# Filter and row loads moved to ScalarE's queue, and unread products cut into quarters of the array

## The chip, the cores and the metric

The kernel runs on one core of a Trainium2 chip. The time is that of the device, in microseconds (us), from the first to the last instruction of one execution. TensorE (PE) multiplies matrices, VectorE (DVE), ScalarE (ACT) and GpSimd (POOL) do element-wise work, and SyncE (SP) issues transfers. ScalarE and GpSimd issue transfers as well, each from its own instruction queue, in the order of its instructions.

## The reference

```python
def _attn_ref(x, filt_r, filt_i):            # x: (8, 3136, 256), filters: (1569, 256)
    X = np.fft.rfft(x, axis=1)
    F = (filt_r + 1j * filt_i)[None, :, :]
    return np.fft.irfft(X * F, n=x.shape[1], axis=1).astype(np.float32)

def _moe_ref(x, w_in, w_out, g_ln):          # x: (25088, 256), w_in: (256, 1024), w_out: (1024, 256)
    h = x @ w_in
    e = np.exp(h - np.max(h, axis=-1, keepdims=True))
    solu = h * (e / (np.sum(e, axis=-1, keepdims=True) + 1e-09))
    mu = np.mean(solu, axis=-1, keepdims=True)
    var = np.mean((solu - mu) ** 2, axis=-1, keepdims=True)
    ln = (solu - mu) / np.sqrt(var + 1e-06) * g_ln
    return (ln @ w_out).astype(np.float32)
```

The first function filters each of 8 entries along its 3136 positions; the second is applied to all 8 x 3136 = 25088 rows of the result.

## The kernel before

The Fourier transform of length 3136 is done in two stages, 49 x 64, as products with tables. `first` multiplies a piece of x (98 rows of 4 x 256 values, loaded by `fetch_x`) by the first table (PE `pa`), and `store_first` writes the result to d1 in device memory. `forward` multiplies a unit of d1 (read by `fetch` as t2) by the second table (PE `pb`), `turn` and `multiply` apply the filters (DVE `p`, `i`), `inverse` goes back (PE `pc`), and `store` writes to d2. `fetch_back` loads a piece of d2 and `back` multiplies it by the last table (PE `py`), which gives `y`, the input of the second function. The second function's products are PE `m` (with w_in) and PE `o` (with w_out).

The 8 entries are taken in five groups. Group 0 is done alone, ahead of everything else. It ends with ten products whose result nobody reads, and with the last table's products for entry 0:

```python
        start(0)
        for i in range(NS):
            sp.turn(i)
            sp.multiply(i, (0, 1))
            if i + 1 < NS:
                start(i + 1)
            last = sp.prods[i]
            sp.inverse(i, nc.scalar.copy)
            sp.store(i, nc.gpsimd.dma_start)

        for j in range(10):
            idle = ps_h.tile([P, 2, 512], FP32, name=f"idle_{j}", tag="h")
            nc.tensor.matmul(out=idle[:, 0, :], lhsT=tables[NS // NG - 1][:, 0, 0, :],
                             rhs=last.rearrange("p b c -> p (b c)"), start=True, stop=True)
        for j in (4, 5):
            begin(j)
        for ch in range(NH // NCH):
            fetch_back(0, ch, pools["r"])
            for cb in range(KD):
                back(0, ch, cb, nc.scalar.copy)
        # ... (the last weights are converted)
```

The loads of the row pieces, from SyncE, and of the filters for groups 1 to 4, from GpSimd:

```python
        def fetch_x(self, i, split=by_16):
            b, ch = divmod(i, NH // NCH)
            self.xs[i] = self.pools["r"].tile([P, NCH, C], FP32, name=f"x_{self.n}_{i}", tag="r")
            split((nc.sync.dma_start, nc.sync.dma_start), self.xs[i][0:NR],
                  x[self.entries[b]].rearrange("(r n) c -> r n c", n=NH)[
                      :, NCH * ch:NCH * ch + NCH, :])

    def fetch_back(e, ch, rows_pool, split=by_16):
        n, b = next((n, g[0].index(e)) for n, g in enumerate(GROUPS) if e in g[0])
        t4s[e, ch] = rows_pool.tile([P, NCH, C], FP32, name=f"t4_{e}_{ch}", tag="r")[0:NK]
        split(
            (nc.sync.dma_start, nc.sync.dma_start), t4s[e, ch],
            d2[n][b].rearrange("s (a n) c -> (s a) n c", a=4)[:, NCH * ch:NCH * ch + NCH, :])

    def load_filter(s, count):
        f = fpool.tile([P, 2, 2, C], FP32, name=f"f_{s}", tag="f")
        for p in range(2):
            nc.gpsimd.dma_start(out=f[NQ * p:NQ * p + NQ, 0:count],
                                in_=f_dram[s:s + count].rearrange("s q k c -> q s k c"))
        return f
```

After that come 196 steps (and a tail), one for each 128 rows of the second function. Two steps make a pair: 7 products with w_in and 28 with w_out. The work of groups 1 to 4 is spread over the steps. In a step `t` with a piece of x or of d2, its products run; in a step with a unit of a spectrum, `pb` runs, and `pc` one step later. All loads of pieces share three buffers (pool "r"), so a load is placed at the end of step `at`, which depends on when the piece three places back is used:

```python
        for i, t in enumerate(spread(pieces, *first_at)):
            row_loads.append((t, lambda sp=sp, i=i: sp.fetch_x(i, whole)))
            # ... first, store_first
        for i, t in enumerate(spread(len(sp.units), *spectrum_at)):
            ahead(t, 2).append(lambda sp=sp, i=i: sp.fetch(i, nc.scalar.dma_start))
            ahead(t, 1).append(lambda sp=sp, i=i: sp.fetch_filter(i))
            ahead(t, 2).append(lambda sp=sp, i=i: sp.fetch_de(i))
            # ... forward and turn in step t, multiply and inverse in t + 1, store in t + 2
    # ...
            row_loads.append((t, lambda e=e, ch=ch: fetch_back(e, ch, pools["r"], whole)))
    # ...
    row_loads.sort(key=lambda load: load[0])
    for n, (t, load) in enumerate(row_loads):
        at = max(t - 3, row_loads[n - 3][0] if n >= 3 else -1)
        assert at < t
        if at < 0:
            load()
        else:
            loads[at].append(load)
```

The order inside a step, cut to what matters here (`first_of` holds the products of pieces in the first nine steps, `early` and `late` hold them afterwards; `keep` and `keep_out` are ScalarE's copies of m and o):

```python
    def step(k):
        # ...
        for job in stores[k] + products[0][k] + first_of[k]:
            job()
        # product(j, 1), keep, project(p, 5), keep_out, product(j, 2)   (even k; odd: product(j, 5), keep)
        # turn(k - 3), regroup(j - 3, 0): SyncE's transfers solu_t<-turn
        # ... finish: VectorE's part of m and o
        exponential(k - 2)                       # ScalarE
        for job in early[k]:
            job()
        # ... the other products, regroup(j - 3, 1), project_sums: GpSimd's additions
        normalize(k - 2)                         # VectorE, then a square on ScalarE
        # ... finish, store_out: SyncE's transfers out_dram<-ot
        for job in mid[k] + late[k] + loads[k]:
            job()
```

Of the kernel before, what the change touches and what calls it, by code (L numbers as in the profile page):

```python
# [24 lines left out]
NS, NQ = (N1 + 1) // 2, 64  # L25
NR = 2 * N1
NK = 4 * NS
NG = 5
# [52 lines left out]
def kernel(  # L81
# [10 lines left out]
    nc = tc.nc  # L92
# [5 lines left out]
    def pool(name, bufs, space=None, stack=ctx):  # L98
        kw = {} if space is None else {"space": space}
        return stack.enter_context(tc.tile_pool(name=name, bufs=bufs, **kw))  # L100
# [51 lines left out]
    class Spectrum:  # L152
# [14 lines left out]
                return ap[:, s, :, :].rearrange("b p c -> p b c")  # L167
            return ap[0, s:s + count, :, :].rearrange("s p c -> p s c")

        def fetch_x(self, i, split=by_16):  # L170
            b, ch = divmod(i, NH // NCH)
            self.xs[i] = self.pools["r"].tile([P, NCH, C], FP32, name=f"x_{self.n}_{i}", tag="r")
            split((nc.sync.dma_start, nc.sync.dma_start), self.xs[i][0:NR],
                  x[self.entries[b]].rearrange("(r n) c -> r n c", n=NH)[
                      :, NCH * ch:NCH * ch + NCH, :])

# [84 lines left out]

    t4s = {}

    def fetch_back(e, ch, rows_pool, split=by_16):

        n, b = next((n, g[0].index(e)) for n, g in enumerate(GROUPS) if e in g[0])
        t4s[e, ch] = rows_pool.tile([P, NCH, C], FP32, name=f"t4_{e}_{ch}", tag="r")[0:NK]
        split(
            (nc.sync.dma_start, nc.sync.dma_start), t4s[e, ch],
            d2[n][b].rearrange("s (a n) c -> (s a) n c", a=4)[:, NCH * ch:NCH * ch + NCH, :])  # L270

    def back(e, ch, cb, evac):

        ps = ps_t.tile([P, 512], FP32, name=f"py_{e}_{ch}_{cb}", tag="t")
        psv = ps[:, 0:NCH * NR].rearrange("p (n r) -> p n r", r=NR)
        for i in range(NCH):
            nc.tensor.matmul(out=psv[:, i, :], lhsT=t4s[e, ch][:, i, cb * P:cb * P + P],  # L277
                             rhs=wi_t, start=True, stop=True)
        n0, t0 = NCH * ch, e % 2 * S
        evac(out=y[:, cb, t0:t0 + S].rearrange("p (r n) -> p n r", n=NH)[:, n0:n0 + NCH, :], in_=psv)  # L280


    with ExitStack() as st:
        pools = {name: pool(name + "0", bufs, stack=st)
                 for name, bufs in (("r", 6), ("t1", 4), ("t2", 5), ("p", 2), ("g", 3))}
# [34 lines left out]
        filters, tables = {}, {}  # L320
# [28 lines left out]
        sp = Spectrum(0, pools, resident, lambda s, count: tables[s // NG][:, s % NG:s % NG + count])  # L349
# [27 lines left out]
        for i in range(NS):  # L377
# [4 lines left out]
            last = sp.prods[i]  # L382
# [2 lines left out]

        for j in range(10):
            idle = ps_h.tile([P, 2, 512], FP32, name=f"idle_{j}", tag="h")
            nc.tensor.matmul(out=idle[:, 0, :], lhsT=tables[NS // NG - 1][:, 0, 0, :],
                             rhs=last.rearrange("p b c -> p (b c)"), start=True, stop=True)
        for j in (4, 5):  # L390
            begin(j)
        for ch in range(NH // NCH):
# [3 lines that stand above are left out]
# [10 lines left out]
    def psum(kind, name):  # L406
        return {"b": ps_b, "t": ps_t}[kind].tile([P, 2, C], FP32, name=name, tag=kind)
# [7 lines left out]
    pools = {name: pool(name + "1", bufs)  # L415
             for name, bufs in (("r", 3), ("t1", 3), ("t2", 2), ("p", 2), ("g", 2))}
# [3 lines left out]
    def load_filter(s, count):  # L420
        f = fpool.tile([P, 2, 2, C], FP32, name=f"f_{s}", tag="f")
        for p in range(2):
            nc.gpsimd.dma_start(out=f[NQ * p:NQ * p + NQ, 0:count],
                                in_=f_dram[s:s + count].rearrange("s q k c -> q s k c"))
        return f

# [223 lines left out]
    def spread(count, start, over):  # L650
        return [start + i * over // count for i in range(count)]

    def ahead(t, by):
        return loads[max(0, t - by)]
# [9 lines left out]
    row_loads = []  # L664

    for n in range(1, len(GROUPS)):
        entries, first_at, spectrum_at = GROUPS[n]
        sp = Spectrum(n, pools, load_filter, load_de)
        pieces = len(entries) * NH // NCH
        for i, t in enumerate(spread(pieces, *first_at)):  # L670
            row_loads.append((t, lambda sp=sp, i=i: sp.fetch_x(i, whole)))
            for u in range(2):
                (first_of if t < LAG else (early, late)[u])[t].append(lambda sp=sp, i=i, u=u: sp.first(
                    i, (u,), psum("t", f"pa_{sp.n}_{i}_{u}").rearrange("p a c -> p (a c)").rearrange(
                        "p (o n) -> p o n", o=1), nc.scalar.copy))
                (first_of[t] if t < LAG else mid[t] if u == 0 else stores[t + 1]).append(
                    lambda sp=sp, i=i, u=u: sp.store_first(i, 2 * u, nc.gpsimd.dma_start))
# [4 lines that stand above are left out]
            early[t].append(lambda sp=sp, i=i: sp.forward(i, psum("b", f"pb_{sp.n}_{i}")))  # L682
            early[t].append(lambda sp=sp, i=i: sp.turn(i, bufs=1))
            for part in range(2):
                products[part][t + 1].append(lambda sp=sp, i=i, part=part: sp.multiply(i, (part,)))
            late[t + 1].append(lambda sp=sp, i=i: sp.inverse(i, nc.scalar.copy))
            stores[t + 2].append(lambda sp=sp, i=i: sp.store(i, nc.gpsimd.dma_start))
    for e in range(1, B):


        start, end = (-(-S * (e - 1) // P) + 1) // 2 * 2 + (2 if e == 3 else 0), S * e // P // 2 * 2 - 2
        for ch, t in enumerate(spread(NH // NCH, start, end - start)):
            row_loads.append((t, lambda e=e, ch=ch: fetch_back(e, ch, pools["r"], whole)))
            for cb in range(KD):
                (first_of if t < LAG else (early, late)[cb])[t].append(
                    lambda e=e, ch=ch, cb=cb: back(e, ch, cb, nc.scalar.copy))
# [133 lines left out]
```

## Time and profile before

| | |
|---|---|
| time, median of 3 runs | 1791.7 us (1790.85 to 1792.85) |
| span of the profiled run | 1779.0 us |
| PE busy | 1671.6 us, 94% |
| DVE, ACT, POOL busy | 1244.1, 1068.4, 1093.9 us |
| mean DMA throughput | 177 GB/s, 314.57 MB |
| filter loads f<-f_dram, GpSimd | 152, 128 or 256 KB each |
| piece loads in the steps, SyncE | 48 of x (392 KB), 56 of d2 (400 KB) |
| unread products | 10, as 20 records, 8.7 us busy by the page's groups |

A profile's page gives busy times and their share of the span, then the span in 40 equal slices, each digit being tenths of a slice (9 is 90% or more). "PEclk" is the granted clock of TensorE in tenths of full speed. The chain follows the work that ended last backwards, at each step to what released it. A line of a group reads: source line, engine, operation, output<-inputs, shape, count, busy time, mean ns of one, idle time ahead of it and who ended that. A line of a timeline starts with start and length in us, and ends with the idle time before it and its releaser. Matmul records overlap, since a matmul's record includes its latency: the rate is read from start to start. An fp32 product of 512 columns is two records. Names like t, d, f and x are the tiles' names without numbers; t<-d is a piece or a unit that is read back, f<-f_dram a filter load.

### The profile page before, as it was taken

What the parts mean: (1) busy time and instruction counts of PE and PEld (TensorE: products, weight loads), DVE (VectorE), ACT (ScalarE), POOL (GpSimd) and SP (SyncE); (2) the same over time, 40 slices, a digit from 0 to 9 for tenths busy, and PEclk for the clock granted to TensorE, in tenths of its full rate; (3) what the DMA queues carried; (4) which work ended last, traced back from release to release, by engine and by line L of the source; (5) the groups of instructions that cost most, each with busy time, mean ns of one, the idle gap of its engine ahead of it and who ended that gap; (6) DMA issues with size and microseconds to landing.
All of it is one profiled execution on the core that took longest, in us unless ns stands there. A gap on an engine that the chain in (4) does not pass through costs nothing.

```text
span 1779.0 us, 28627 instructions
## 1 busy us (share of the span) xinstructions
PE 1671.6 (94%) x8692; PEld 1141.3 (64%) x8692; DVE 1244.1 (70%) x2586; ACT 1068.4 (60%) x1917; POOL 1093.9 (61%) x1290
## 2 busy tenths in 40 slices
PE   6688887899999999999999999989999999999996
PEld 1225445676666666766667667767777777777776
DVE  0793654578877875678798766767767777777773
ACT  2365555566767666666667666656666566655551
POOL 3242354677767775667877656546666656676664
PEclk9789998999999999999999999999999999999999
DMA  9876687897788865566777665557776444444443
GB/s 279 259 253 184 207 216 197 245 247 211 201 240 231 223 173 158 135 188 188 195 188 200 156 153 157 139 141 186 192 188 158 113 116 114 120 106 107 104 114 94
DMA packets 358120, 314.57 MB, mean 177 GB/s; under 512 B 60833, under 2 KB 318882, under 8 KB 357968
## 3 DMA queue, kind: packets, MB, share of 16 engines
q1 hardware_dynamic: 295664, 187.23, 41.0%
q0 software_dynamic: 29152, 86.45, 16.3%
q10 hardware_dynamic: 33152, 39.07, 7.7%
q8 instruction: 71, 1.16, 0.3%
q14 instruction: 81, 0.66, 0.1%
HBM read 131.65 MB, written 81.50 MB: 120 GB/s over the span
## 4 chain that ended last, share of the span: by engine, by line
PE 74%; DMA 11%; DVE 6%; ACT 3%; issue 3%; SPq 1%; POOL 1%; ACTq 0%; POOLq 0%; DVEq 0%
PE o L612 28%; PE m L500 28%; PE py L277 6%; PE pa L183 4%; PE pb L210 4%; PE pc L252 3%; DMA t<-d 2%; DMA x<-in_x_dram 2%; DMA d<-t 2%; DVE h L548 1%; DMA solu_t<-turn 1%; DMA f<-f_dram 1%; DMA de<-de_tbl 1%; ACT e L532 1%; DVE i L242 1%
## 5 line engine op out<-in xcount | busy, mean ns | idle before, releaser
L550 ACT ACTIVATE e<-h,nmu 128x1024 f32<-128x1024 f32 x196 | 225.3, 1150 | 307.9 <-DVE h L548 305.7
L612 PE MATMUL o<-w_out_sb,solu_t 128*128 128x128 f32 x3136 | 401.9, 277 | 3.0 <-DVE ot L629 1.9
L612 PEld LDWEIGHTS o<-w_out_sb,solu_t 128*128 128x128 f32 x3136 | 382.1, 193 | 33.6 <-issue 28.5
L500 PE MATMUL m<-w_in_sb,s 128*128 128x512 f32 x784 | 397.3, 598 | 6.3 <-ACT h L510 6.3
L612 PEld LDWEIGHTS o<-w_out_sb,u 128*128 128x128 f32 x2352 | 306.5, 192 | 148.7 <-issue 115.7
L612 PE MATMUL o<-w_out_sb,u 128*128 128x128 f32 x2352 | 312.7, 276 | 9.0 <-ACT ot L624 7.7
L479 POOL TENSOR_TENSOR u<-solu_t 128x512 f32<-128x512 f32 x98 | 153.9, 1571 | 265.8 <-DMA solu_t<-turn 152.3
L500 PE MATMUL m<-w_in_sb,y 128*128 128x512 f32 x588 | 304.5, 601 | 6.3 <-DVE h L521 3.5
L548 DVE SCALAR_TENSOR_TENSOR h<-e,rsum,h 128x1024 f32<-128x1024 f32 x196 | 291.8, 1489 | 7.1 <-DVE rsum L545 0.3
L631 DVE SCALAR_TENSOR_TENSOR ot<-o,rs_t,ot 128x128 f32<-128x128 f32 x294 | 102.5, 349 | 257.3 <-ACT ot L624 216.6
L479 POOL TENSOR_TENSOR u<-solu_t,u 128x512 f32<-128x512 f32 x98 | 144.7, 1477 | 173.1 <-PE o L612 171.6
L558 DVE STREAM_TRANSPOSE turn<-h 128x1024 f32<-128x1024 f32 x196 | 242.2, 1236 | 1.5
L524 DVE CUSTOM_DVE_ANT_0 h<-m,h 128x512 f32<-128x512 f32 x196 | 134.8, 688 | 138.3 <-ACT h L510 89.8
L510 ACT COPY h<-m 128x512 f32<-128x512 f32 x294 | 173.0, 589 | 91.3 <-PE m L500 77.9
L532 ACT ACTIVATE e<-h,nmax 128x1024 f32<-128x1024 f32 x196 | 224.5, 1146 | 0.0
L500 PEld LDWEIGHTS m<-w_in_sb,s 128*128 128x128 f32 x784 | 130.6, 192 | 79.2 <-issue 74.2
L277 PEld LDWEIGHTS py<-wi_t,t 100*128 100x128 f32 x1024 | 133.3, 195 | 62.9 <-issue 39.8
L183 PE MATMUL pa<-x,wf_t 98*100 98x512 f32 x256 | 141.7, 662 | 26.6 <-DMA x<-in_x_dram 20.7
L479 POOL TENSOR_TENSOR solu_t<-solu_t,solu_t 128x512 f32<-128x512 f32 x98 | 157.0, 1602 | 7.7
L277 PE MATMUL py<-wi_t,t 100*128 100x98 f32 x1024 | 134.9, 277 | 15.2 <-DMA t<-d 10.4
L500 PEld LDWEIGHTS m<-w_in_sb,y 128*128 128x128 f32 x588 | 99.3, 192 | 74.2 <-issue 50.8
L280 ACT COPY y<-py 128x392 f32<-128x392 f32 x128 | 108.2, 845 | 56.2 <-PE py L277 54.6
(72 smaller groups left out, 2049.1 us busy)
## 6 DMA issues: line engine op xcount, KB each, us to landing
solu_t<-turn SPq DMA_DIRECT2D x784, 128.0 KB
d<-g POOLq DMA_DIRECT2D x99, 256.0 KB, 5.5
out_dram<-ot SPq DMA_DIRECT2D x196, 128.0 KB
t<-d SPq DMA_DIRECT2D x56, 400.0 KB
d<-t POOLq DMA_DIRECT2D x96, 200.0 KB, 4.8
t<-d ACTq DMA_DIRECT2D x74, 256.0 KB
x<-in_x_dram SPq DMA_DIRECT2D x48, 392.0 KB
f<-f_dram POOLq DMA_DIRECT2D x104, 128.0 KB, 4.2
```

The costliest lines, as they stand in the source:

```text
L183: nc.tensor.matmul(out=ps[0:NK, j], lhsT=wf_t, rhs=self.xs[i][0:NR, 2 * u:2 * u + 2, :], start=True, stop=True)
L277: nc.tensor.matmul(out=psv[:, i, :], lhsT=t4s[e, ch][:, i, cb * P:cb * P + P], rhs=wi_t, start=True, stop=True)
L280: evac(out=y[:, cb, t0:t0 + S].rearrange("p (r n) -> p n r", n=NH)[:, n0:n0 + NCH, :], in_=psv)
L479: nc.gpsimd.tensor_tensor(out=out, in0=in0, in1=in1, op=op)
L500: nc.tensor.matmul(out=ms[j, bank], lhsT=lhsT, rhs=w_in_sb[:, w, :], start=m in (1, 2, 7), stop=True, skip_group_check=True)
L510: nc.scalar.copy(out=h_half(k, i), in_=ms[j, 0])
L524: nc.vector.tensor_tensor_reduce(out=h_half(k, i), in0=ms[j, bank], in1=h_half(*kept), scale=1.0, scalar=sofar, op0=ALU.add, op1=ALU.min, ...
L532: nc.scalar.activation(out=e, in_=hs[k], func=AFT.Exp, bias=nmaxs.pop(k)[:, 1:2], scale=-1.0, accum_out=esum)
L548: nc.vector.scalar_tensor_tensor(out=solu, in0=e, scalar=rsum, in1=solu, op0=ALU.mult, op1=ALU.mult, accum_out=nmu)
L550: nc.scalar.activation(out=e, in_=solu, func=AFT.Square, bias=nmu, scale=-float(DFF), accum_out=variances[g][:, i:i + 1])
L558: nc.vector.transpose(out=turns[g][:, :, i, :], in_=solus.pop(k).rearrange("p (f j) -> p f j", j=32))
L612: nc.tensor.matmul(out=pos[p, bank], lhsT=lhs[:, f, :], rhs=w[:, f, :], start=f == 0 and m in (1, 2, 7), stop=True, skip_group_check=True)
```

## The change

Three things change. The pieces of x and of d2 that are loaded in the steps, and the filters of groups 1 to 4, are issued from ScalarE's queue in place of SyncE's and GpSimd's, which frees SyncE's queue for the regrouping and the output and GpSimd for its additions. And each of the ten unread products, which keep TensorE busy until the first piece is back, becomes four products on 64 x 64 quarters of the array, with the two halves of rows going to different PSUM banks.

```diff
-        def fetch_x(self, i, split=by_16):
+        def fetch_x(self, i, split=by_16, dma=nc.sync.dma_start):
...
-            split((nc.sync.dma_start, nc.sync.dma_start), self.xs[i][0:NR],
+            split((dma, dma), self.xs[i][0:NR],
...
-    def fetch_back(e, ch, rows_pool, split=by_16):
+    def fetch_back(e, ch, rows_pool, split=by_16, dma=nc.sync.dma_start):
...
-            (nc.sync.dma_start, nc.sync.dma_start), t4s[e, ch],
+            (dma, dma), t4s[e, ch],
...
             idle = ps_h.tile([P, 2, 512], FP32, name=f"idle_{j}", tag="h")
-            nc.tensor.matmul(out=idle[:, 0, :], lhsT=tables[NS // NG - 1][:, 0, 0, :],
-                             rhs=last.rearrange("p b c -> p (b c)"), start=True, stop=True)
+            for r in (0, NQ):
+                for c in (0, NQ):
+                    nc.tensor.matmul(out=idle[c:c + NQ, r // NQ, :],
+                                     lhsT=tables[NS // NG - 1][r:r + NQ, 0, 0, c:c + NQ],
+                                     rhs=last[r:r + NQ].rearrange("p b c -> p (b c)"),
+                                     start=True, stop=True)
...
-            nc.gpsimd.dma_start(out=f[NQ * p:NQ * p + NQ, 0:count],
+            nc.scalar.dma_start(out=f[NQ * p:NQ * p + NQ, 0:count],
...
-            row_loads.append((t, lambda sp=sp, i=i: sp.fetch_x(i, whole)))
+            row_loads.append((t, lambda sp=sp, i=i: sp.fetch_x(i, whole, nc.scalar.dma_start)))
...
-            row_loads.append((t, lambda e=e, ch=ch: fetch_back(e, ch, pools["r"], whole)))
+            row_loads.append((t, lambda e=e, ch=ch: fetch_back(e, ch, pools["r"], whole, nc.scalar.dma_start)))
```

The pieces of entries 0 and 1 for group 0 and the pieces read back for entry 0 keep SyncE's queue.

## The prediction

> **What bounds the kernel now.** I read the page first: the busy shares, the slices and the chain.
>
> ```profile
> PE 1671.6 (94%) x8692; PEld 1141.3 (64%) x8692; DVE 1244.1 (70%) x2586; ACT 1068.4 (60%) x1917; POOL 1093.9 (61%) x1290
> ...
> PE   6688887899999999999999999989999999999996
> ...
> PEclk9789998999999999999999999999999999999999
> DMA  9876687897788865566777665557776444444443
> ...
> PE 74%; DMA 11%; DVE 6%; ACT 3%; issue 3%; SPq 1%; POOL 1%; ACTq 0%; POOLq 0%; DVEq 0%
> ```
>
> TensorE is the bound from the ninth slice on. Before that its digits are 6 to 8 and the DMA digits are as high as 9. The busy time by stretches says how much idle time there is to win (columns: stretch, its length, then busy us of PE, PEld, DVE, ACT and POOL, the granted clock, DMA share, GB/s):
>
> ```profile
> 225.00:270.00 45.00, 37.50 (x142) 19.67 (x140) 24.13 (x51) 26.36 (x47) 28.25 (x37) 1.00 0.92 230
> 270.00:315.00 45.00, 36.74 (x173) 25.87 (x173) 22.24 (x46) 23.21 (x44) 20.57 (x29) 0.89 0.73 200
> ...
> 1000.00:1100.00 100.00, 98.78 (x555) 69.96 (x554) 66.24 (x145) 61.54 (x113) 59.01 (x70) 1.00 0.59 151
> 1100.00:1200.00 100.00, 92.80 (x532) 68.78 (x531) 64.68 (x144) 59.12 (x107) 55.34 (x66) 0.97 0.54 139
> ```
>
> Subtracting PE busy from the length in all stretches: 39.5 us idle before 135 us, 13.3 from 135 to 225, 20.5 from 225 to 360, 19.3 in the 1340 us from 360 to 1700, 14.8 at the end. The first and last of these hold none of the moved loads. So the **ceiling of any gain** is 13.3 + 20.5 + 19.3 = 53 us, 3% of the span, and a gain over 2% would need two thirds of it.
>
> **Where the filters cost something.** The largest single hole of the long stretch is at 1178 to 1185 us. The timeline there, GpSimd then VectorE then TensorE:
>
> ```profile
> 1175.18 1.37 POOL L479 TENSOR_TENSOR u<-solu_t 128x512 f32<-128x512 f32 x1 [10.35 <-DMA solu_t<-turn]
> ...
> 1177.83 1.31 POOL L423 DMA_DIRECT2D f<-f_dram  x2
> ...
> 1184.66 0.69 DVE L238 TENSOR_TENSOR p<-pb,f 128x512 f32<-128x512 f32 x1 [7.74 <-DMA f<-f_dram]
> ...
> 1185.45 2.05 PE L210 MATMUL pb<-t,de 128*128 128x256 f32 x4 [7.20 <-issue]
> ```
>
> GpSimd sat 10.35 us in an addition that waited for a regrouping transfer; the filter load behind it in the same queue went out late, VectorE could not read pb, and TensorE could not overwrite it. In the waits, "DVE p L238 <- DMA f<-f_dram" is 25.8 us over 12 times. Of PE's holes after 360 us that I can trace to it, this one is 7.2 us and one at 785 us 1.1. The granted clock is half in the stretch 1182.2 to 1189, so the 3.6 us of products after the hole also run at half speed: 1.8 us lost.
>
> **What the Trainium skill says.** (1) "TensorE: Matmul & The Clock Gate", Part 1: after about 3.4 us without work the clock falls to half. The trace agrees: PE idle from 276 to 283.64 us, granted clock 0.51 in the stretch 281 to 285. (2) The same page, Part 3, "What overlaps and what doesn't": matmuls on different parts of the array run side by side, but they start and end in strict order. No tiled product is in this trace. (3) "DMA: Bandwidth & Descriptors", "Issuing engines are not separate DMA queues": transfers of all issuers share the same 16 engines, and another issuer saves only the time of issuing. The trace fits: at a DMA share of 0.92 (225 to 270 us) a new queue adds no bandwidth.
>
> **Part A, the unread products.** They stand between the last inverse product and the first product that uses a row piece read back:
>
> ```profile
> 140.96 8.75 PE L388 MATMUL idle<-p,de 128*128 128x512 f32 x20
> ...
> 149.55 16.40 PE L277 MATMUL py<-wi_t,t 100*128 100x98 f32 x128
> ```
>
> Ten products are 20 records (each fp32 product is two), one every 0.43 us: 8.6 us, and the next stage starts right at their end, so every us more here is a us more in the span. The change makes 40 products, 80 records of 512 columns. If the two records of one quarter must follow each other but the next quarter starts beside the second (order kept, as in (2)), a quarter costs one 0.43 us: 40 x 0.43 = 17.2 us, **+8.6 us**. If nothing overlaps: 80 x 0.43 = 34.4, +25.8. If all four quarters overlap fully: about 8.6, +0. I give these 0.5, 0.3 and 0.2 and put +8.6 into the sum.
>
> **Part B, row pieces from ScalarE's queue.** 104 pieces (48 of x, 56 read back) leave SyncE, where they waited for their buffer and went out the moment it was free. On ScalarE they stand at the end of a step, behind its exponential, square and copies. From the built order of the changed kernel and the program's rule for `at`: of 104 pieces 67 are issued at the end of step t-3 and are safe; 8 go out only one place ahead of their step, three of them before the first step and five at the end of step t-1, just before use. The first example is the third piece of x. Before, SyncE issued it at 168.00 and TensorE used it at once when it got there:
>
> ```profile
> 168.00 2.10 SPq L144 DMA_DIRECT2D x<-in_x_dram  x2
> ...
> 179.79 0.59 ACT L510 COPY h<-m 128x512 f32<-128x512 f32 x1 [1.91 <-PE m L500]
> 180.45 1.88 PE L183 MATMUL pa<-x,wf_t 98*100 98x512 f32 x4
> ```
>
> In the new order it comes after that copy at 179.79. From issue to first use such a piece took 4 to 6 us where PE waited for it (241.91 to 248.18 on the chain is 6.1, 143.9 to at most 149.55 for the first piece read back is 5.6); with 4.5 it lands near 184.5 and PE loses 4. By the same reading the sixth piece (issued behind the square that ends at 198.9, wanted at 199.5) loses 4.5, and the second piece of the next group (behind 224.0, wanted at 224.6) 4. Two more later (steps 11 and 14) perhaps 2 each. Three gaps over 3.4 us cost some 1.7 us of half clock each, 5. Together 21.5; but PE in this stretch already loses 13.3 us waiting for copies behind stores, and a hole made earlier fills part of those. I count a little over half: **+12 us**. Against it, the piece at step 11 went out late from SyncE before (on the chain "271.02 12.49 DMA t<-d", PE stopped 7.5 us); there DMA is saturated and the new place is no earlier, so I take no gain.
>
> **Part C, ScalarE's time and new coupling.** Issues have durations:
>
> ```profile
> L461 ACTq DMA_DIRECT2D de<-de_tbl x76: 326/482/2255, 238.4 to 1348.1; - x76
> ...
> L144 SPq DMA_DIRECT2D t<-d x56: 281/492/1231, 157.1 to 1528.1; - x56
> L144 SPq DMA_DIRECT2D x<-in_x_dram x48: 316/342/1305, 155.4 to 1108.7; - x48
> ```
>
> Added to ScalarE: 56 x 0.49 + 48 x 0.34 = 44 us of rows, and 152 filter loads at about 0.38 (the median of its own loads of t) = 58 us: 102 us over some 1375. Its busy share of about 0.7 plus 0.1 of issuing in the steps with a spectrum becomes about 0.9, of which another 0.05 to 0.1 must stay free because the square waits for VectorE every step ("ACT e L550 <- DVE h L548", 305.7 us). ScalarE waits for TensorE 77.9 us in its copies of m, so most of it hides; an issue also runs while the arithmetic before it still does. The second cost is in the built program: the hardware queues of SyncE and ScalarE share eight completion semaphores in turn, so a transfer may not be issued before the one eight places back has landed. ScalarE's transfers of the long part wait for one of SyncE's about 110 times in the old program and 240 times in the new. A late regrouping transfer then holds ScalarE, and with it the copies TensorE needs. I put **+5 us**, with a tail to +20.
>
> **Part D, gains.** The filters no longer stand behind GpSimd's additions: 7.2 + 1.1 us of holes and 1.8 of half clock. Rows no longer stand behind stores on SyncE: a hole of 2.0 at 702 us before products on a piece read back. Together **-12 us**. GpSimd is also relieved of 152 x 0.569 = 86 us ("L423", 86.2) and SyncE of its 97.9 us of waiting for TensorE in row loads; TensorE waits for GpSimd's sums only 1.3 us in all, so neither shortens the span by itself.
>
> **Sum.** +8.6 + 12 + 5 - 12 = +13.6 us. Because D may be larger where GpSimd is also late before 360 us (10 of the 12 filter waits are not counted above), I set +8: 1791.7 + 8 = **1800 us**.
>
> **The rivals.** *First: relief wins.* Filters and regrouping transfers arrive early, B is hidden because the DMA engines, not the order, set the pace before 360 us: A alone is paid, D and perhaps 15 more of the 20.5 us in 225 to 360 come back: about 1770. For it: the DMA share of 0.92 and 0.73 there; against it: a saturated DMA moves the same bytes either way. *Second: ScalarE becomes the bound.* It blocks in issues behind landings, PE waits for copies of m and o in every spectrum step: 76 such steps at 0.4 us are +30, with the rest about 1830. For it: the doubled waits on shared semaphores; against it: in the old trace the copies of m waited for transfers only 4 us in all. *Third: quarters run one after the other*: +17 on top, about 1817.
>
> **Range and chances.** The three rivals bound it: 1772 to 1834 for 8 in 10. Faster by over 2% (below 1756) needs 36 of the 53 us of idle time with A free: 0.04. Slower by over 2% (above 1827.5) needs serial quarters together with costly B, or a bound ScalarE: 0.16. Within 2%: 0.80.
>
> **What would show it.** A: the span of the idle group and the start of the py products after it (158 us for 17.2). B: "PE pa <- DMA x" waits at the third and sixth pieces near 185 to 215 us, and half-clock stretches there. C: ScalarE's gaps before its transfer issues, PE waits on "ACT h" and "ACT ot" in 360 to 630 us. D: "DVE p <- DMA f" near zero and no hole near 1185. I am wrong if PE's idle time from 360 to 1700 us grows instead of shrinking, or if B does not appear although the pieces go out late.

## The result and the profile after

The changed kernel takes 1852.31 us (median), the kernel before 1791.28 us in the runs beside it. The ratio is 1.035, with a 95% interval of 1.030 to 1.040: slower by some 63 us. The prediction said 1800 us and a range up to 1834.

The page of the changed kernel, same lines as shown of the one before (busy shares, slices of TensorE and its granted clock, the chain):

```profile
PE 1693.0 (91%) x8752; PEld 1144.5 (62%) x8752; DVE 1228.1 (66%) x2586; ACT 1062.7 (57%) x1917; POOL 992.9 (54%) x1138
...
PE   5688877689998999999999999999999999999996
...
PEclk9799888899999999999999999999999999999999
...
PE 64%; DMA 14%; ACT 7%; DVE 7%; issue 4%; ACTq 2%; POOL 1%; SPq 1%; DVEq 0%; POOLq 0%
```

TensorE's share of the chain falls from 74% to 64%. ScalarE's arithmetic rises from 3% to 7% and its issuing (ACTq) from 0% to 2%: the chain now runs through ScalarE. The same four stretches as before (stretch, length, busy us of PE, PEld, DVE, ACT, POOL, granted clock, DMA share, GB/s):

```profile
225.00:270.00 45.00, 34.30 (x102) 17.44 (x101) 17.95 (x38) 23.43 (x40) 19.64 (x29) 0.85 0.64 172
270.00:315.00 45.00, 30.36 (x131) 20.47 (x132) 19.87 (x43) 19.31 (x37) 14.61 (x19) 0.81 0.64 181
1000.00:1100.00 100.00, 98.95 (x526) 66.94 (x525) 79.89 (x161) 65.27 (x121) 59.88 (x65) 1.00 0.63 173
1100.00:1200.00 100.00, 100.00 (x562) 71.17 (x561) 65.00 (x145) 63.20 (x116) 57.95 (x73) 1.00 0.61 160
```

The first two rows lost products and clock, and their DMA share fell from 0.92 and 0.73 to 0.64: TensorE does not wait there for want of DMA throughput. The last row has what part D promised: no hole near 1185 us, TensorE busy 100.00 of 100 us where it was 92.80. Taken the way the prediction took it (length less PE busy), the idle time from 360 to 1700 us grew from 19.3 to 51.3 us. That was the prediction's own sign that it is wrong. Following each step's exponential in both traces, the changed kernel is 8 us late at step 2, 28 at step 14, 43 at step 20 and 70 at step 44; after that the difference hardly grows. The steps up to 20 hold the early row pieces, and 76 of the 152 filter loads go out before 700 us, that is up to about step 46.

TensorE's waits in the whole trace (engine, line, what it waited for: us in total, times, longest):

```profile
PE pa L183 <- DMA x<-in_x_dram: 36.1, 16, 7.3
PE m L504 <- ACT h L514: 31.4, 23, 8.6
PE o L616 <- ACT ot L628: 27.7, 35, 2.4
```

Before, the first of these was 20.7 us, and the two waits for ScalarE's copies 6.3 and 7.7. ScalarE copies m to h and o to ot so that TensorE may overwrite the PSUM tile. One such wait, in ScalarE's timeline (start, duration, instruction; "ACTq" is the issue of a transfer):

```profile
580.95 1.48 ACTq L427 DMA_DIRECT2D f<-f_dram  x2
582.52 1.71 ACTq L197 DMA_DIRECT2D t<-d  x1
584.27 0.51 ACTq L465 DMA_DIRECT2D de<-de_tbl  x1
584.82 0.42 ACTq L144 DMA_DIRECT2D t<-d  x1
585.29 0.59 ACT L514 COPY h<-m 128x512 f32<-128x512 f32 x1 [6.06 <-DMA f<-f_dram]
```

Two filter loads, a load of t, one of de and a row piece stand in a row at the end of the step: ScalarE's queue is taken from 580.95 to 585.24, and only then comes the copy. The "6.06" is ScalarE's idle time ahead of the copy. Issuing is not counted as busy: 4.3 us of it are these issues, and the 1.7 us ahead of them ScalarE waited until an older transfer had landed. The filter load is named as the cause, but the copy needs no filter. TensorE stands still for that copy:

```profile
586.02 1.45 PE L504 MATMUL m<-w_in_sb,s 128*128 128x512 f32 x2 [3.09 <-ACT h L514]
```

The same place in the kernel before, at another unit:

```profile
401.15 0.38 ACTq L197 DMA_DIRECT2D t<-d  x1
401.57 0.48 ACTq L461 DMA_DIRECT2D de<-de_tbl  x1
402.09 0.59 ACT L510 COPY h<-m 128x512 f32<-128x512 f32 x1 [0.40 <-PE m L500]
```

Summed over the 76 units, ScalarE's idle time ahead of the first copy of m behind a unit's loads is 33 us before (0.44 us each, part of it the issues) and 171 us after.

### The profile page after: what moved, and what is told of

Same layout as the page of the kernel before. It is cut to its first block, busy times and chain, and to the rows that moved or that the text cites. A ratio compares the mean times of both kernels' runs of the same rounds, so it can differ in the third digit from the quotient of the medians.

```text
span 1853.4 us, 28544 instructions
## 1 busy us (share of the span) xinstructions
PE 1693.0 (91%) x8752; PEld 1144.5 (62%) x8752; DVE 1228.1 (66%) x2586; ACT 1062.7 (57%) x1917; POOL 992.9 (54%) x1138
## 4 chain that ended last, share of the span: by engine, by line
PE 64%; DMA 14%; ACT 7%; DVE 7%; issue 4%; ACTq 2%; POOL 1%; SPq 1%; DVEq 0%; POOLq 0%
PE o L616 25%; PE m L504 24%; PE py L277 5%; PE pa L183 4%; DMA solu_t<-turn 3%; PE pc L252 3%; DMA x<-in_x_dram 3%; DMA f<-f_dram 3%; ACT e L536 2%; DMA t<-d 2%; PE pb L210 2%; DMA rs_t<-rows 2%; DMA d<-t 1%; DVE h L552 1%; ACTq L427 1%
## 5 line engine op out<-in xcount | busy, mean ns | idle before, releaser
L504 PE MATMUL m<-w_in_sb,s 128*128 128x512 f32 x784 | 406.9, 611 | 32.0 <-ACT h L514 31.4
L616 PE MATMUL o<-w_out_sb,u 128*128 128x128 f32 x2352 | 317.0, 278 | 29.5 <-ACT ot L628 27.7
L483 POOL TENSOR_TENSOR u<-solu_t 128x512 f32<-128x512 f32 x98 | 143.3, 1462 | 323.2 <-DMA solu_t<-turn 189.2
L552 DVE SCALAR_TENSOR_TENSOR h<-e,rsum,h 128x1024 f32<-128x1024 f32 x196 | 280.0, 1428 | 7.1 <-DVE rsum L549 0.2
L483 POOL TENSOR_TENSOR u<-solu_t,u 128x512 f32<-128x512 f32 x98 | 155.6, 1588 | 182.0 <-PE o L616 180.6
L504 PEld LDWEIGHTS m<-w_in_sb,y 128*128 128x128 f32 x588 | 100.8, 194 | 76.0 <-issue 45.3
L260 POOL DMA_DIRECT2D d<-g x101 | 76.5, 757 | 130.5 <-ACT g L255 122.3
L483 POOL TENSOR_TENSOR solu_t<-solu_t,solu_t 128x512 f32<-128x512 f32 x98 | 139.1, 1420 | 7.7
```

What stands on the lines that cost most here:

```text
L483: nc.gpsimd.tensor_tensor(out=out, in0=in0, in1=in1, op=op)
L504: nc.tensor.matmul(out=ms[j, bank], lhsT=lhsT, rhs=w_in_sb[:, w, :], start=m in (1, 2, 7), stop=True, skip_group_check=True)
L552: nc.vector.scalar_tensor_tensor(out=solu, in0=e, scalar=rsum, in1=solu, op0=ALU.mult, op1=ALU.mult, accum_out=nmu)
L616: nc.tensor.matmul(out=pos[p, bank], lhsT=lhs[:, f, :], rhs=w[:, f, :], start=f == 0 and m in (1, 2, 7), stop=True, skip_group_check=True)
```

## The experiments

Each run has a ratio to the kernel before, timed on the same chip. Two more columns come from the traces. "Copies" is TensorE's waits for ScalarE's copies of m and o, the two rows above added. "Landings" is ScalarE's idle time ahead of an issue whose wait names the very semaphore that the transfer will signal: it waits there until an older transfer with that semaphore has landed (from the instruction records after 150 us, gaps over 0.15 us).

| kernel | us, median | ratio (95% interval) | copies, us | landings, us |
|---|---|---|---|---|
| before | 1786 to 1791 | 1 | 14.0 | 2.1 |
| the whole change | 1852.3 | 1.035 (1.030 to 1.040) | 59.1 | 53.3 |
| quarters alone | 1784.6 | 0.999 (0.996 to 1.002) | 12.8 | 4.4 |
| filters alone | 1826.5 | 1.022 (1.018 to 1.027) | 37.4 | 15.6 |
| rows alone | 1807.1 | 1.011 (1.006 to 1.015) | 18.6 | 27.0 |
| filters from SyncE | 1869.8 | 1.045 (1.040 to 1.051) | 12.2 | 0.7 |
| copies in place of filter issues | 1844.4 | 1.031 (1.025 to 1.037) | 48.8 | 3.5 |
| filters in mid-step, ScalarE | 1794.0 | 1.004 (1.002 to 1.006) | 21.2 | 17.9 |
| copies in mid-step | 1811.2 | 1.014 (1.010 to 1.017) | 31.1 | 1.4 |
| late rows alone | 1773.1 | 0.992 (0.990 to 0.994) | 14.4 | 12.6 |
| filters in mid-step, GpSimd | 1783.6 | 0.999 (0.997 to 1.002) | 15.8 | 9.7 |
| the change repaired | 1812.5 | 1.013 (1.010 to 1.015) | 43.2 | 45.3 |
| late rows and copies in mid-step | 1805.3 | 1.011 (1.008 to 1.013) | 39.7 | 6.3 |
| what gains, together | 1776.7 | 0.992 (0.990 to 0.995) | 16.1 | 21.3 |

One of the four executions with the filters from SyncE ran at a lower granted clock than the others and is left out. Costs in us below are the ratio less one, times 1790.

The theories: **first**, issuing takes ScalarE's time at a place where TensorE's copies stand behind it; **second**, row pieces go out too late; **third**, the transport itself, that is the hardware queue and its shared completion semaphores.

### The parts alone

**Quarters alone.** Only the matmul lines of the change.

> The kernel before with only the unread products as four quarters. Full overlap (the trace of the changed kernel has the 80 records within about 9.6 us, where 20 took 8.7): the group costs about 1 us more, the time is 1792 us, within 0.2% of before. Part A of the prediction (half overlap): 1800. Serial quarters: 1817. If the product group is dearer than its span, because the clock is at half behind it or the row stage after it starts late, it is above 1795.

Measured: no difference that can be seen, -2 us (-7 to +3). Full overlap.

**Filters alone.**

```diff
-            nc.gpsimd.dma_start(out=f[NQ * p:NQ * p + NQ, 0:count],
+            nc.scalar.dma_start(out=f[NQ * p:NQ * p + NQ, 0:count],
```

> The kernel before with only the filters issued by ScalarE. First theory, ScalarE's time: two filter issues of about 0.6 us stand at the end of each of 76 steps ahead of the copies that TensorE waits for, and ScalarE then also waits for landings; the loss lies between 180 and 700 us, about 35 to 45 of the 61 us, so 1825 to 1837, with the hole near 1185 us gone (the step times after 1000 us come back by about 7). Second theory, late row pieces: the filters are a gain, 1780 to 1790, and the whole loss is in the rows. Third theory, the completion semaphores and the hardware queue as such: the same 1825 to 1837 here, and the same again with the filters issued by SyncE.

Measured: +40 us, two thirds of the loss, as the first and third theory had it. In its waits (us, times, longest) TensorE waits for ScalarE's copies where it hardly did before:

```profile
PE o L612 <- ACT ot L624: 24.3, 34, 1.8
...
PE m L500 <- ACT h L510: 13.1, 15, 1.8
```

**Rows alone.** Only the `fetch_x` and `fetch_back` lines of the change.

> The kernel before with only the row pieces issued by ScalarE. First theory, ScalarE's time: 104 issues of 0.34 to 0.49 us, mostly before 700 us, 15 to 20 us of late pieces up to step 14 and some 5 from issue time: 1807 to 1815. Second theory, late row pieces carry nearly all of it: 1835 or more. If the two parts only hurt together (ScalarE has room for either alone), this and the filters alone both stay under 1805.

Measured: +19 us. The parts add up to -2 + 40 + 19 = 57 us, the whole change is 63 (54 to 71): the three parts account for it. The step times say where the rows lose: 15 us at step 2, 33 at step 18, 41 at step 42, and 7 us come back between steps 112 and 122. From 150 to 400 us TensorE's waits for x are

```profile
PE pa L183 <- DMA x<-in_x_dram: 16.3, 4, 7.4
```

against 3.9 us in the kernel before.

**Filters from SyncE.** The same line with `nc.sync`.

> The kernel before with the filters issued by SyncE instead of GpSimd: the same hardware queue kind and the same shared semaphores, but no compute engine pays for the issue. First theory, ScalarE's time: nothing is lost, the hole near 1185 us is gone, 1779 to 1790. Third theory, transport: 1825 or more, as with the filters from ScalarE. A fourth possibility: filters now stand in order behind row pieces and regrouping transfers that wait for buffers in SyncE's queue, and VectorE waits for filters: 1795 to 1815 with waits of VectorE for f above the 25.8 us of before.

Measured: +81 us, dearer than ScalarE. The third theory's number, but not on ScalarE: it waits 0.7 us for landings, and TensorE 12.2 for copies, no more than before. What grew is VectorE's waits for the filters (us, times, longest):

```profile
DVE p L238 <- DMA f<-f_dram: 118.1, 41, 6.9
```

It was 25.8 us, and GpSimd's waits for regrouping transfers (u <- solu_t) went from 152.3 to 205.1 us. In SyncE's queue the filters stand behind regrouping loads that wait for their data, and these behind the filters. That is the fourth possibility of the expectation, which I had given at most 25 us. But the third theory's mechanism is in this trace too, in SyncE's own queue:

```profile
SPq L423 <- DMA t<-d: 53.4, 20, 10.1
```

Ahead of 20 filter issues SyncE stood still for 53.4 us in all until a load of t had landed that ScalarE had issued: the two had the same completion semaphore. How the 81 us divide between order and landings is not shown. So the run doesn't clear the transport; it takes the runs that follow.

### ScalarE's time, and its place

**Copies in place of the filter issues.** Filters stay with GpSimd; six small copies, each 128x32, stand where the two issues stood.

```diff
             nc.gpsimd.dma_start(out=f[NQ * p:NQ * p + NQ, 0:count],
...
+            for _ in range(3):
+                nc.scalar.copy(spare, spare)
```

> The kernel before, filters still issued by GpSimd, with six small ScalarE copies (128x32, about 0.2 us each, 1.2 to 1.6 us a unit) at the very place where the two filter issues of the filters-alone run stood. No transfer is moved. Theory one, ScalarE's time at the end of the step: most of the 39 us of the filters-alone run comes back, 1815 to 1830. Theory three, the hardware queue and its shared completion semaphores: ScalarE had room for this, at most 1797.

Measured: +56 us, with no transfer moved. The copies' row (min/median/max ns):

```profile
L428 ACT COPY spare<-spare x456: 201/218/263, 256.9 to 1429.8; 128x32 f32<-128x32 f32 x152
```

456 x 0.218 = 99 us of ScalarE's time at the end of the step cost 56 us. The filter issues there are 152 of 0.601 us in the median, 89 us in all, and cost 40. So time at that place suffices as the cause.

**Filters in mid-step, from ScalarE.** The same 152 transfers on the same queue, issued right behind the exponential.

```diff
-            ahead(t, 1).append(lambda sp=sp, i=i: sp.fetch_filter(i))
+            in_gap[max(0, t - 1)].append(lambda sp=sp, i=i: sp.fetch_filter(i))
...
-        for job in early[k]:
+        for job in in_gap[k] + early[k]:
```

> As the filters-alone run, the same 152 transfers from ScalarE, but issued right behind the exponential, where ScalarE waits for VectorE anyway (305.7 us of such waits before). Theory one (time at the wrong place in ScalarE's order): the loss falls to a third or less, 1780 to 1800. Theory three (transport, semaphores): as the filters alone, 1820 to 1833. If ScalarE is short of time anywhere in the step, between: 1805 to 1815.

Measured: +6 us in place of +40. Queue, engine and bytes are the same, and by the records 250 of ScalarE's 320 transfers follow one of SyncE's on the same semaphore (214 of 320 with the filters at the end of the step, 122 of 168 before). This takes out the transport as such as the cause of the 40 us. It leaves open how much of the 40 are the 15.6 us for which ScalarE waited for landings at the end of the step; here it waits 17.9 us for them and loses little. In the timeline the issues run beside the exponential:

```profile
585.93 0.45 ACTq L423 DMA_DIRECT2D f<-f_dram  x1
586.25 1.15 ACT L532 ACTIVATE e<-h,nmax 128x1024 f32<-128x1024 f32 x1
586.42 1.03 ACTq L423 DMA_DIRECT2D f<-f_dram  x1
587.31 0.19 ACT L532 ACTIVATION_READ_ACCUMULATOR e<-h,nmax 128x1 f32 x1
```

From 585.93 to 587.45 ScalarE issues twice and computes 1.34 us.

**Copies in mid-step.** The six copies moved to the same place.

> The six small ScalarE copies a unit of the earlier run, moved from the end of the step to the place behind the exponential; no transfer is moved. If the place alone decides (ScalarE waits for VectorE there), the 56 us fall to 0 to 12: 1786 to 1798. If ScalarE's total time decides, the loss stays near 56 us: 1835 or more.

Measured: +24 us, neither number. Moving them takes away over half of the 56, but arithmetic of 1.3 us a unit costs four times what the issues of 1.2 us cost there. Place decides most, and issues are cheaper there than arithmetic of the same length, which fits with their running beside the exponential.

### The rows, and the change repaired

**Late rows alone.** Pieces wanted from step 22 on from ScalarE, earlier ones from SyncE.

```diff
+                i, whole, nc.scalar.dma_start if t >= 22 else nc.sync.dma_start)))
```

> As the rows-alone run, but pieces wanted before step 22 stay in SyncE's queue; the later ones are ScalarE's. Theory two for the rows (late pieces in the first steps, part B): nearly the whole 19 us is gone, 1786 to 1793. If the issue time of rows costs as the filters' does: 1797 to 1803, growing between steps 20 and 44.

Measured: -14 us (-18 to -10), better than both numbers. The early pieces alone therefore cost 19 + 14 = 33 us (about 24 to 42, the two intervals combined). In its trace the hole that part D named is down to 1.4 us, and the one at 702 us is gone:

```profile
1100.00:1200.00 100.00, 98.50 (x572) 72.95 (x571) 67.23 (x150) 63.85 (x115) 64.21 (x77) 1.00 0.58 152
```

92.80 has become 98.50, although the filters are still GpSimd's: with the rows out of SyncE's queue GpSimd's longest wait for a regrouping load around 1180 us is 6.2 us and not 10.3. Between steps 112 and 122 this trace gains 7.4 us on the one before. Where the rest of the 14 us comes from can't be read from one pair of traces, since the profiled execution of the kernel before (1779.0 us) is itself shorter than its median.

**Filters in mid-step, from GpSimd.** The mid-step edit alone.

> The kernel before with the filters still from GpSimd, but issued in the middle of the step instead of at its end, ahead of the addition that waited 10.35 us at 1175 us. If the gain of part D (9 us of late filters) can be had without ScalarE: 1776 to 1783, no hole near 1185 us. If the issue instead takes GpSimd time ahead of sums that TensorE wants: 1788 to 1800.

Measured: -1 us (-6 to +3). The hole near 1185 us is gone (98.02 us busy from 1100 to 1200) and no gain can be seen in the time. The hole is no accident of one execution: the trace of quarters alone has it too, with 7.8 us. So either it isn't worth its 7 us in the median time, or the new place of the issues in GpSimd's queue takes them back; the run doesn't tell which.

**The change repaired.** The whole change with filters in mid-step and early rows from SyncE.

> The whole change, quarters, filters and rows, with two repairs: the filters go out behind the exponential, and row pieces wanted before step 22 stay with SyncE. If the two causes found are all of the 61 us, the parts add up: -1 (quarters) +6 (filters in the gap) -10 to -14 (late rows) = 1775 to 1784. If the parts hurt each other in ScalarE's queue (more landings waited for), 1795 to 1810.

Measured: +22 us, where the parts give -2 + 6 - 14 = -10. The second number was right: they hurt each other. One of the new holes, ScalarE's timeline:

```profile
598.22 0.19 ACT L536 ACTIVATION_READ_ACCUMULATOR e<-h,nmax 128x1 f32 x1
603.11 1.10 ACTq L427 DMA_DIRECT2D f<-f_dram  x2
604.31 0.59 ACT L221 ACTIVATE i<-pb 64x512 f32<-64x512 f32 x1 [5.90 <-DMA solu_t<-turn]
```

and TensorE's:

```profile
606.65 2.04 PE L616 MATMUL o<-w_out_sb,u 128*128 128x128 f32 x8 [5.43 <-ACT ot L628]
```

The records behind them: SyncE issued a regrouping load at 595.64 that signals semaphore 112; its last piece landed at 603.03, after all others by 600.53; the filter load that signals 112 too was issued at 603.11. ScalarE did nothing for 4.7 us, because a load that it doesn't need had not landed. That is the third theory's mechanism, shown here for one hole.

**Late rows and copies in mid-step.** Late rows from ScalarE, filters from GpSimd, the six copies in mid-step: ScalarE's time without the filters' semaphores.

> Late row pieces from ScalarE, filters from GpSimd, and the six small ScalarE copies a unit in the middle of the step: the repaired change with its filter issues replaced by pure ScalarE time, so without their use of completion semaphores. The repaired change took 1812 where its parts alone added up to 1781. If ScalarE's time, crowded by rows and filters together, is the reason, this is as slow or slower, 1812 or more, as the copies alone cost more than the issues alone did (1811 against 1794). If the reason is that ScalarE's transfers wait for landings, nothing hurts jointly here: -14 for the rows and +22 for the copies, 1793 to 1803.

Measured: +19 us, between the two numbers. The parts give -14 + 24 = +10, so 9 us (about 1 to 17) are hurt jointly without any filter transfer on ScalarE; with the transfers it was 22 + 10 = 32 us (about 23 to 41). So ScalarE's time alone hurts jointly, and the larger part comes only with the filter transfers, where landings are 45.3 us and not 6.3. That landings are this larger part is likely, not shown: the best version, below, waits 21.3 us for them and loses nothing. How the 23 us divide over single holes isn't settled.

**What gains, together.** Quarters, late rows from ScalarE, filters in mid-step from GpSimd.

> Quarters, late rows from ScalarE, early rows from SyncE, filters from GpSimd in the middle of the step: what is left of the change that gains. Sum of the single runs: -2 - 13 - 1, so 1768 to 1776. If the gain of the late rows and of the filters in the middle is the same hole near 1185 us, it is the late rows' alone, 1771 to 1778.

Measured: 1776.7 us, -14 us (-19 to -9): the best version, with late rows alone. It is faster than both kernels. The other two edits add nothing that can be seen.

## Why the prediction was wrong

**The step that failed is part C**, ScalarE's time, put at +5 us with a tail to 20; the filters alone cost 40 (33 to 47). Two things went wrong in it. The smaller is the size of the issues: a filter load was taken from ScalarE's own loads of t, 0.38 us, and it is

```profile
L427 ACTq DMA_DIRECT2D f<-f_dram x152: 452/594/2653, 265.8 to 1430.5; - x152
```

0.594 in the median, while the load of t behind it went from 0.377 to 0.598 (with the filters in mid-step it takes 0.377 again). ScalarE's issues after 150 us grew from 72 to 218 us, 146 and not 102. The larger is the sentence that most of it hides, since ScalarE waits 77.9 us for TensorE in its copies of m. Those waits are spread over all copies of m; where the loads stand, ahead of the first copy behind them, ScalarE had 0.44 us a unit, and two filter issues take 1.2. The prediction compared a sum of busy time with a sum of waiting time over all steps, and had known from the code that the loads stand at the end of the step, right ahead of the next copies. The two runs with copies show how much place is worth: 99 us of work cost 56 at the end of the step and 24 in the middle.

The rival "ScalarE becomes the bound" had the mechanism and nearly the size: it gave 0.4 us for each of 76 steps, and the filters alone measured 40 / 76 = 0.53. I discounted it because in the old trace the copies waited only 4 us for transfers, which said nothing of a queue that didn't yet hold the loads. The Trainium skill, "DMA: Bandwidth & Descriptors", "Issuing engines are not separate DMA queues", says that another issuer saves only the issue time, "which is usually small relative to the DMA itself". The runs do not bear out the "only": late rows gained 14 us and filters lost 81 by the queue they stood in. And small against a transfer is not small for the engine that pays it, 0.594 us ahead of a copy of 0.59.

The shared completion semaphores, the other half of part C, are at most a part of what the filters alone lost, by the mid-step run. In the whole change ScalarE waits 53.3 us for landings. The repaired version shows, for one hole, that such a wait reaches TensorE once both kinds of load are in ScalarE's queue.

**Part B** had the mechanism and places right, and its size wrong: +12 predicted, about 33 measured. The third piece of x is issued at

```profile
181.90 0.77 ACTq L144 DMA_DIRECT2D x<-in_x_dram  x2
```

behind the copy of m, and TensorE gets it late by what was predicted (4 us):

```profile
186.63 3.08 PE L183 MATMUL pa<-x,wf_t 98*100 98x512 f32 x4 [3.92 <-DMA x<-in_x_dram]
```

What failed is "a little over half" of a list of 21.5 us, and in the list the clock. The list had 16.5 us of waits and 5 of half clock. The same two stretches before and in rows alone (granted clock third from the end):

```profile
150.00:225.00 75.00, 64.36 (x285) 37.87 (x284) 29.39 (x81) 43.28 (x66) 20.55 (x37) 0.95 0.63 190
225.00:360.00 135.00, 114.52 (x492) 72.66 (x491) 71.29 (x140) 74.98 (x135) 76.97 (x103) 0.94 0.84 224
```

```profile
150.00:225.00 75.00, 64.06 (x256) 38.90 (x255) 18.71 (x58) 31.16 (x46) 15.79 (x28) 0.82 0.52 160
225.00:360.00 135.00, 106.68 (x404) 64.65 (x403) 63.66 (x134) 69.11 (x122) 61.77 (x85) 0.86 0.66 189
```

From the first product on a piece read back to the exponential of step 24, rows alone took 29.7 us longer than the kernel before. In that time TensorE was idle 14.4 us longer, and it was busy 33.4 us longer at half clock, which costs half of that, 16.7 us; the two together come within 1.4 us of the whole. So the list's waits were about right in sum, and the clock cost three times its 5 us. (Among the traces that leave the early rows with SyncE, the clock's cost in this part differs by up to 7 us.) The prediction let the clock fall only after 3.4 us without work. In rows alone 13.7 us at half clock from 166.6 us on follow an idle time of 1.15 us, and in the kernel before 3.4 us from 206.0 on follow one of 2.24 us. The list also left out that ScalarE is held at such an issue: in the trace of the whole change it waits 4.9 us at 297 us and 6.4 us at 304 us for landings before a row piece.

**Part A** was +8.6 and is nothing:

```profile
144.28 9.79 PE L390 MATMUL idle<-p,de 64*64 64x512 f32 x80
154.00 16.50 PE L277 MATMUL py<-wi_t,t 100*128 100x98 f32 x128
```

80 records span 9.79 us where 20 took 8.75, and the next stage starts at 154.00 and not at 158. The one microsecond more is not the quarters': half clock until 146.3 us falls into the group, as it does in rows alone, where the 20 whole records take 9.82 us. I had given full overlap 0.2. The Trainium skill, "TensorE: Matmul & The Clock Gate", Part 3, "Measured speedup vs the span model", has the span of packed products as one product and some 4 ns for each further one; this trace agrees, with 2 to 7 ns from start to start in each group of four records. The prediction rested on the section before that one and halved the overlap for the second record of an fp32 product.

**Part D**, -12, was about right in size by luck: the late rows alone gain 14, but of the 12 the prediction had put 10 down to the filters and 2 to the rows. Its reason is only half borne out. The hole near 1185 us closes with the filters moved and also with the rows moved, so it is had once; and closing it from GpSimd's own queue gained nothing that can be seen. What gains is to take late rows out of SyncE's queue.

The sum as measured is -2 (A) + 33 (B) + 40 (C, less the hole that the filters close too) - 14 (D) = 57, and the whole change is 63.

## What to carry to other kernels

The cost of a transfer issue is decided by what stands behind it in the issuing engine's order, not by that engine's busy share: look in its timeline for the next instruction that another engine waits for, and count issue time and waits for landings ahead of it in full. If an engine waits for others somewhere in each step, issue there, beside long arithmetic, and measure it together with whatever else goes into that queue: here parts that added up to -10 us came to +22. Before moving loads as a group, split them by how soon they are wanted: here the late ones gained 14 us and the early ones lost 33.

## What the runs showed of the hardware

- Four fp32 products on 64x64 quarters take the time of one whole product: 80 records in 9.79 us, 20 in 9.82 (the whole change and rows alone); records of a group of four start 2 to 7 ns apart.
- An issue on ScalarE runs beside its arithmetic: 1.2 us of issues a unit cost 6 us in 1790 in mid-step, 1.3 us of arithmetic 24.
- SyncE has no arithmetic to hold up, yet 152 loads added to its queue cost 81 us: an engine that only issues still orders its transfers, and it waits for landings too (53.4 us for loads of t).
- Half clock does not need 3.4 us without work: 13.7 us of it follow an idle time of 1.15 us in rows alone.
- ScalarE's load of t takes 0.377 us to issue, and 0.598 right behind two filter loads.
- One piece of a regrouping load landed 2.5 us after the rest (603.03 against 600.53) and held ScalarE for an unrelated load.
